# Two overlapped attention branches on one core: fewer filler matmuls, a signal per score matmul, and work of the last stage moved forward

## The chip, the cores and the metric

One core of one Trainium2 chip. The metric is device time of one execution in microseconds. The kernel before takes 1512.03 us (median of 4, 1510.74 to 1512.83).

The engines: PE multiplies matrices, DVE is the vector engine, ACT the scalar engine (exponentials), POOL a third elementwise engine, SP issues DMAs. In this kernel each has a list of instructions of its own, and one waits for another through semaphores.

## The reference, cut

Two branches on separate inputs, both with S = 2048, D = 512, 32 heads of 16.

```python
def _A_ref(x, wqkv, wo):              # ordinary softmax attention
    q, k, v = ...                     # x @ wqkv, split in heads
    scores = jnp.einsum("bhqd,bhkd->bhqk", q, k) * Dh ** -0.5
    p = _softmax(scores, axis=-1)
    o = jnp.einsum("bhqk,bhkd->bhqd", p, v)
    return o.reshape(B, S, D) @ wo

def _B_ref(x, wqkv, w_phi, wo):       # linear attention with learned feature maps
    q, k, v = ...
    pq, pk = q @ w_phi, k @ w_phi     # per head, 16 x 16
    phi_q = concat([softmax(pq), softmax(-pq)]); phi_k = the same of pk
    kv = einsum("bhsf,bhsd->bhfd", phi_k, v);  z = phi_k summed over s
    o = (phi_q @ kv) / (phi_q @ z + 1e-6)
    return o.reshape(B, S, D) @ wo

out = concat([A, B], axis=-1)
```

## The kernel before

**The loop.** Branch A runs in 1024 slots, 32 to a unit (a group of four heads and 512 queries). A slot does two things for different units: the first pass, two score matmuls (L561) and DVE's row-max over 128 x 1024 of them (L573); and, 43 slots later, the second pass, two score matmuls with the maximum folded in (L642), ACT's exponential of each (L654), and every other slot four P·V matmuls (L669). The second pass has three score banks in PSUM.

```python
def emit_m2(B):
    n, bank, dep = ring_next()                     # one of banks 4, 5, 6
    m2_t[B] = P.op("pe", lambda e: e.matmul(PS[:, bank, :], KT[...], QT[...], ...),
        [dep, qe_t[u], kt_ready[(g, kt // 4)]], signal=(B % 2 == 1))
    if B % 2 == 1:
        m2_t[B - 1] = m2_t[B]                      # both exponentials wait for the second
```

PE also runs `emit_fill`: groups of four matmuls of zeros, which compute nothing. Each slot is filled up to `NCOL = 3` columns of work. Once in a unit, `emit_qb` broadcasts the row maxima through PE into one of the three score banks, for two to three slots; the X copy empties the P·V bank; and ACT does two Ln and two Exp of the denominators.

```python
for tau in range(last_slot + 1):
    if tau < total_q1: emit_m1(tau)                # first pass
    ... emit_m2, emit_exp of slot tau - 43 ...     # second pass
    ... P·V, broadcast, hooks of branch B ...
    if tau < total_q1 + LAG and ncol < NCOL:
        emit_fill(NCOL - ncol)
    if tau < total_q1: emit_r1(tau)                # DVE row max
```

**The tail.** In the last 43 slots there is no first pass, so DVE is free. There, hooks (functions tied to a slot) compute branch B's key feature maps, one per 128 rows, three slots apart (`e_k0` to `e_k4`: PE; DVE max, min and two subtractions; ACT exp; DVE sum and reciprocal; POOL product; PE). After the last slot come A's sixteen output projections, a wait on all engines (`endA`), and the final stage: sixteen query feature maps (`q_f0` to `q_f3`, the same arithmetic) in a software pipeline with the query product and B's output projection (`q_s0` to `q_s3`).

```python
for st in range(NKT):
    base = T0 + 3 + 3 * st
    for off, fn in ((0, e_k0), (1, e_k1), (2, e_k2), (3, e_k3), (5, e_k4)):
        tail_hooks.setdefault(base + off, []).append(lambda st=st, fn=fn: fn(st))
...
for st in range(NKT):                              # A's output projection, after attention
    ... 8 matmuls into one bank; copy by ACT or DVE in turn; DMA out ...
endA = [last_tok(k) for k in ("pe", "act", "dve", "pool")]
```

## Time and profile before

| | before |
|---|---|
| loop ends (last row max) | 1282.7 us |
| a unit of 32 slots | 38.01 us |
| tail | 228.4 us |
| of that DVE busy / not busy | 158.7 / 69.6 us |

An engine's reported busy time contains the end of an operation that overlaps the next one's start. Where operations follow one another without a wait, the spacing of their starts is what one costs: a row max is reported at 1.22 us and costs 1.131; a 512-column exponential is reported at 0.60 and costs 0.49. In a timeline line, the first column is the start, the second the stretch covered by the "x" operations named at its end, and the bracket the idle time before them with what ended it. PEclk is the granted PE clock as a share of full.

### The profile page before, as it was taken

To read this page: it belongs to the slowest core of one execution; us is meant where nothing else is said; L and a number is where in the kernel's file an instruction comes from. 1 tells how busy PE (TensorE), PEld (TensorE's weight loads), DVE (VectorE), ACT (ScalarE), POOL (GpSimd) and SP (SyncE) were. 2 spreads that over 40 slices of the span, in tenths; PEclk is the share of its full clock that TensorE was granted. 3 is DMA by queue.
4 is the path that set the end of the run, shared out by engine and by line. 5 is a ranking of instruction groups with operands and counts; after the bars stand their busy time and mean duration, and the time that the engine had idled before them with its cause. 6 is when DMAs were issued, how large, how long until landed. Compare 5 with 4: busy or idle time off the path is not lost.

```text
span 1511.1 us, 40934 instructions
## 1 busy us (share of the span) xinstructions
PE 1404.6 (93%) x18220; PEld 468.5 (31%) x18220; DVE 1353.5 (90%) x1341; ACT 1301.8 (86%) x2466; POOL 157.0 (10%) x257
## 2 busy tenths in 40 slices
PE   3999999999999999999999999999999999897766
PEld 1433333333333333333333333333333333332333
DVE  3399999999999999999999999999999999575598
ACT  2648999999999999999999999999999999883256
POOL 4000000000000000000000000000000000243143
PEclk9999999999999999999999999999999999997879
DMA  5006000000000000000000000000000000000101
GB/s 111 1 1 127 20 5 6 5 6 5 5 5 6 5 5 5 5 5 6 5 5 5 6 6 5 5 6 5 6 5 5 5 5 5 5 2 15 46 18 39
DMA packets 34513, 20.47 MB, mean 14 GB/s; under 512 B 25120, under 2 KB 31776, under 8 KB 34336
## 3 DMA queue, kind: packets, MB, share of 16 engines
q1 hardware_dynamic: 34336, 17.86, 5.4%
q8 instruction: 142, 2.33, 0.6%
q14 instruction: 35, 0.29, 0.1%
HBM read 4.21 MB, written 4.19 MB: 6 GB/s over the span
## 4 chain that ended last, share of the span: by engine, by line
PE 75%; ACT 13%; DVE 9%; SPq 2%; issue 1%; POOL 0%; DMA 0%; DVEq 0%; ACTq 0%; POOLq 0%
PE PS L685 31%; PE PS L561 19%; ACT pT L654 10%; PE PS L669 9%; PE PS L642 5%; PE PS L274 4%; PE PS L804 2%; DVE part L573 2%; SPq L174 1%; DVE VP L421 1%; PE PS L696 1%; ACT ebK L412 1%; ACT X L706 1%; PE PS L256 1%; PE PS L391 1%
## 5 line engine op out<-in xcount | busy, mean ns | idle before, releaser
L573 DVE TENSOR_REDUCE part<-PS 128x2 f32<-128x1024 f32 x1024 | 1181.9, 1219 | 82.5 <-PE PS L561 55.4
L654 ACT ACTIVATE pT<-PS 128x512 bf16<-128x512 f32 x2048 | 1115.7, 600 | 51.9 <-PE PS L642 39.8
L685 PE MATMUL PS<-zmv,ones_t 128*32 128x512 bf16 x9176 | 665.8, 381 | 0.0
L642 PE MATMUL PS<-QT,KT 32*128 32x512 bf16 x2048 | 464.8, 385 | 11.7 <-ACT pT L654 5.7
L561 PE MATMUL PS<-KT,QT 32*128 32x512 bf16 x2048 | 397.4, 385 | 0.1
L685 PEld LDWEIGHTS PS<-zmv,ones_t 128*32 128x32 bf16 x9176 | 205.0, 96 | 199.4 <-issue 101.4
L561 PEld LDWEIGHTS PS<-KT,QT 32*128 32x128 bf16 x2048 | 96.4, 91 | 430.4 <-issue 256.5
L669 PE MATMUL PS<-pT,VP 128*32 128x512 bf16 x2048 | 205.0, 390 | 13.3 <-ACT X L706 13.3
L642 PEld LDWEIGHTS PS<-QT,KT 32*128 32x128 bf16 x2048 | 124.8, 91 | 66.1 <-ACT pT L654 37.5
L730 POOL TENSOR_TENSOR QT<-X,Yd 128x256 bf16<-128x256 f32 x64 | 46.5, 727 | 786.4 <-ACT Yd L728 786.4
L669 PEld LDWEIGHTS PS<-pT,VP 128*32 128x32 bf16 x2048 | 52.6, 92 | 131.7 <-issue 109.4
L274 PE MATMUL PS<-xAT,WKp 128*128 128x512 bf16 x128 | 35.0, 416 | 22.8 <-DVE WKp L197 17.2
L286 ACT ACTIVATE KT<-PS,bias_k 128x512 bf16<-128x512 f32 x32 | 22.0, 687 | 37.4 <-PE PS L274 37.4
L696 PE MATMUL PS<-zmv,ones_t 128*32 128x512 bf16 x692 | 49.7, 381 | 3.2
L594 POOL TENSOR_SCALAR stage<-mrow 128x16 bf16<-128x16 f32 x32 | 9.9, 310 | 407.9 <-DVE mrow L584 407.9
L378 ACT ACTIVATE VP<-PS 128x1024 bf16<-128x1024 bf16 (+2 forms) x33 | 25.9, 789 | 18.8 <-PE PS L899 15.0
L433 POOL TENSOR_TENSOR QT<-KT,VP 128x512 bf16<-128x512 bf16 x32 | 33.1, 1056 | 80.3 <-DVE VP L424 43.4
L391 PE MATMUL PS<-WKp,xAT 128*128 128x512 bf16 x128 | 39.9, 448 | 0.0
L433 POOL TENSOR_TENSOR phikK<-ebK,statK 128x512 bf16<-128x512 bf16 x32 | 33.1, 1056 | 64.3 <-DVE statK L424 51.2
L282 ACT ACTIVATE QT<-PS 128x512 bf16<-128x512 f32 x32 | 19.1, 597 | 20.9 <-PE PS L274 20.9
L421 DVE TENSOR_REDUCE statK<-ebK 128x64 f32<-128x1024 bf16 x16 | 19.5, 1220 | 18.7 <-ACT ebK L412 18.7
L274 PE MATMUL PS<-xAT,WQp 128*128 128x512 bf16 x128 | 34.0, 389 | 0.0
(79 smaller groups left out, 646.4 us busy)
## 6 DMA issues: line engine op xcount, KB each, us to landing
Yd<-X SPq DMA_DIRECT2D x128, 32.0 KB, 2.0
out_dram<-OA SPq DMA_DIRECT2D x16, 128.0 KB, 1.7
out_dram<-pT SPq DMA_DIRECT2D x16, 128.0 KB, 1.7
wA<-in_A_wqkv_dram SPq DMA_DIRECT2D x3, 512.0 KB, 4.4
wA<-in_B_wqkv_dram SPq DMA_DIRECT2D x1, 1536.0 KB, 8.6
WOp<-in_A_wo_dram SPq DMA_DIRECT2D x4, 128.0 KB, 6.4
BD<-in_B_w_phi_dram SPq DMA_DIRECT2D x32, 0.5 KB, 1.5
woB<-in_B_wo_dram SPq DMA_DIRECT2D x1, 512.0 KB, 4.6
```

Source lines behind the costliest of these rows:

```text
L274: tok = P.op("pe", lambda e, ct=ct: e.matmul(PS[:, b, :], wpad[:, ct, g, :], xAT[:, ct, c * 512:(c + 1) * 512], start=(ct == 0), stop=(ct ...
L391: tok = bank_task(bank, 4, lambda e, b, ct: e.matmul(PS[:, b, :], xBT[:, ct, st * 128:(st + 1) * 128], Wf[:, x, ct, :], start=(ct == 0), s ...
L421: t6 = P.op("dve", lambda e: e.tensor_reduce(ss, ebuf[:, ie, :].rearrange("p (g f) -> p g f", f=16), AX.X, ALU.add), [ctx["exp"]] + users. ...
L433: t8 = P.op("pool", lambda e, a=a: e.tensor_tensor(dv[:, a], ev4[:, a], rs3[:, a].unsqueeze(2).broadcast_to([128, 32, 16]), ALU.mult), [ct ...
L561: tok = P.op("pe", lambda e, r=r: e.matmul(PS[:, r, :], QT[32 * r:32 * r + 32, g, q0:q0 + 128], KT[32 * r:32 * r + 32, g, kc * 512:(kc + 1 ...
L573: r1[q1] = P.op("dve", lambda e: e.tensor_reduce(part[:, u % 2, qt, 2 * half:2 * half + 2, kc], PS[:, 2 * half:2 * half + 2, :], AX.X, ALU ...
L642: m2_t[B] = P.op("pe", lambda e: e.matmul(PS[:, bank, :], KT[32 * r:32 * r + 32, g, kt * 128:(kt + 1) * 128], QT[32 * r:32 * r + 32, g, c ...
L654: exp_t[B] = P.op("act", lambda e: e.activation(pT[:, slot, :], PS[:, bank, :], ACT.Exp, scale=0.25), [m2_t[B], slot_reader.get(slot)])
L669: tok = P.op("pe", lambda e, B=B, r=r: e.matmul(PVB[32 * r:32 * r + 32, :], VP[:, kt, 4 * g + r, :], pT[:, B % RING, :], start=(kt == 0), ...
L685: P.op("pe", lambda e, cq=cq: e.matmul(PVB[32 * cq:32 * cq + 32, :], ones_t[:, 0:32], zmv[:, :], start=False, stop=False, tile_position=(0 ...
L696: P.op("pe", lambda e, cq=cq: e.matmul(PS[32 * cq:32 * cq + 32, bank, :], ones_t[:, 0:32], zmv[:, :], start=True, stop=True, tile_position ...
L730: t = P.op("pool", lambda e: e.tensor_tensor(QT[:, g, lo:lo + 256], X[:, ub, sl], Yd[:, ub, sl], ALU.mult), [ex, xev_t[u], last_m2[u]])
```

## The change

Two small edits in the loop and several in the tail. The intent, in its own words, is to overlap early query feature maps of branch B and A's output projection with attention.

```diff
-    NCOL = 3
+    NCOL = 2
...
-                wB[:], B_wqkv.rearrange(...)), done)                    # B's weights: only the value third
+                wB[:, :, 1024:1536], B_wqkv.rearrange(...)[:, :, 1024:1536]), done)
...
-            ctx["v"] = P.op("act", lambda e: e.activation(               # value copy of a key map
+            ctx["v"] = P.op("dve", lambda e: e.tensor_copy(
...
+        NEQ = 12                      # e_q0..e_q3: twelve query maps, in the key maps' buffers
+        ...                           # their results wait in parts of wB, WQp, phikK, vBK
+        def e_oproj(st): ...          # one output projection; the copy always on DVE
...
-            for off, fn in ((0, e_k0), (1, e_k1), (2, e_k2), (3, e_k3), (5, e_k4)):
+            for off, fn in ((0, e_k0), (1, e_k1), (4, e_k2), (5, e_k3), (7, e_k4)):
+        for j in range(NEQ):
+            base = T0 + 3 + 3 * NKT + 3 * j
+            ...
+        for st in range(12):
+            tail_hooks.setdefault(T0 + 5 + 3 * st, []).append(lambda st=st: e_oproj(st))
+        for st in range(12, 16):
+            tail_hooks.setdefault(32 * (NU - 1) + 90 + 2 * (st - 12), [])...
...
-                [dep, qe_t[u], kt_ready[(g, kt // 4)]], signal=(B % 2 == 1))
+                [dep, qe_t[u], kt_ready[(g, kt // 4)]])                  # every score matmul signals
-                m2_t[B - 1] = m2_t[B]
...
-                ncol += 2                                                # the broadcast's columns
+                ncol += 3
...
-            if tau < total_q1 + LAG and ncol < NCOL:
+            if tau < total_q1 and ncol < NCOL:                           # no fills in the tail
...
-        for st in range(NKT): ...     # the sixteen projections after attention: gone from here
...                                    # q_f0..q_f3 skip st < NEQ and take the early result
```

More of the change, by code (lines that the diff above doesn't have):

```diff
@@ L344, in b_loads @@
             BL["wb"] = P.dma("sp", d_wb, lambda e: e.dma_start(
-                wB[:], B_wqkv.rearrange("(ct p) n -> p ct n", p=128)), done)
+                wB[:, :, 1024:1536], B_wqkv.rearrange("(ct p) n -> p ct n", p=128)[:, :, 1024:1536]), done)
             for x in range(2):
@@ L387, in e_fold, with fm0 @@
             return 1
-        def fm0(st, x, tbuf, sbuf, ctx, bank):
+        def fm0(st, x, tbuf, sbuf, ctx, bank, rk="E"):
             i = ctx["i"]
@@ L396, in fm0 @@
             mn = sbuf[:, i, 32:64]
-            prev = users.get(("mxmn", x, i), []) + users.get(("tb", x, i), [])
+            ctx["rk"] = rk
+            prev = users.get(("mxmn", rk, i), []) + users.get(("tb", rk, i), [])
             t1 = P.op("dve", lambda e: e.tensor_reduce(mx, pv, AX.X, ALU.max), [tok] + prev)
@@ L405, in fm0 @@
             bank_reader[bank] = t4
-            users[("mxmn", x, i)] = [t3, t4]
+            users[("mxmn", rk, i)] = [t3, t4]
             ctx["sub"] = [t3, t4]
@@ L412, in fm1 @@
             ctx["exp"] = P.op("act", lambda e: e.activation(ebuf[:, ie, :], tbuf[:, i, :], ACT.Exp),
-                              ctx["sub"] + users.get(("eb", x, ie), []))
-            users[("tb", x, i)] = [ctx["exp"]]
+                              ctx["sub"] + users.get(("eb", ctx["rk"], ie), []))
+            users[("tb", ctx["rk"], i)] = [ctx["exp"]]
         def fm2(x, ebuf, sbuf, ctx):
@@ L422, in fm2 @@
                 ss, ebuf[:, ie, :].rearrange("p (g f) -> p g f", f=16), AX.X, ALU.add),
-                [ctx["exp"]] + users.get(("ssrs", x, i), []))
+                [ctx["exp"]] + users.get(("ssrs", ctx["rk"], i), []))
             ctx["rs"] = P.op("dve", lambda e: e.reciprocal(rs, ss), [t6])
@@ L435, in fm3 @@
                     [ctx["rs"]] + after)
-            users[("ssrs", x, i)] = [t8]
-            users[("eb", x, ctx["ie"])] = [t8]
+            users[("ssrs", ctx["rk"], i)] = [t8]
+            users[("eb", ctx["rk"], ctx["ie"])] = [t8]
             ctx["phi"] = t8
@@ L447, in e_k0 @@
             vv = vBK[:, st % 4, :].rearrange("p (h j) -> p h j", j=17)
-            ctx["v"] = P.op("act", lambda e: e.activation(
-                vv[:, :, 0:16], PS[:, b, :].rearrange("p (h d) -> p h d", d=16), ACT.Copy),
+            ctx["v"] = P.op("dve", lambda e: e.tensor_copy(
+                vv[:, :, 0:16], PS[:, b, :].rearrange("p (h d) -> p h d", d=16)),
                 [tok, t_vb1] + users.get(("v", st % 4), []))
@@ L481, in e_k4, with e_q0, e_q1, e_q2 @@
             return 1
+        NEQ = 12
+        wTf = WQp[:].rearrange("p a b c -> p (a b c)")
+        vBf = vBK[:].rearrange("p a n -> p (a n)")
+        phiq_slot = {}
+        for j in range(4):
+            phiq_slot[j] = wB[:, j, 0:1024]
+            phiq_slot[4 + j] = wTf[:, 1024 * j:1024 * (j + 1)]
+        phiq_slot[8] = phikK[:, 0, :]
+        phiq_slot[9] = phikK[:, 1, :]
+        phiq_slot[10] = vBf[:, 0:1024]
+        phiq_slot[11] = vBf[:, 1024:2048]
+        qst = {}
+        def e_q0(j):
+            f = NKT + j
+            ctx = qst.setdefault(j, {"i": f % 2, "ie": f % 3})
+            fm0(j, 0, tbK, statK, ctx, early_bank())
+            return 1
+        def e_q1(j):
+            fm1(0, tbK, ebK, qst[j])
+            return 0
+        def e_q2(j):
+            fm2(0, ebK, statK, qst[j])
+            return 0
+        def e_q3(j):
+            after = []
+            if j >= 4:
+                after = list(wf_tok.values())
+            if j >= 8:
+                after = [kst[NKT - 1]["kv"]]
+            fm3(0, ebK, statK, qst[j], phiq_slot[j], after)
+            return 0
+        OA = sb("OA", [128, 2, 512], BF)
+        d_oa = [dsem("oa0"), dsem("oa1")]
+        oa_t = {}
+        def e_oproj(st):
+            c = st // 4
+            b = early_bank()
+            deps = [mul_t[u] for u in range(NU) if units[u][1] == c] + [t_wo, bank_reader.get(b)]
+            tok = None
+            for g in range(NG):
+                tok = P.op("pe", lambda e, g=g: e.matmul(
+                    PS[:, b, :], QT[:, g, st * 128:(st + 1) * 128], WOp[:, g, :],
+                    start=(g == 0), stop=(g == NG - 1)), deps if g == 0 else [], signal=(g == NG - 1))
+            t = P.op("dve", lambda e: e.tensor_copy(OA[:, st % 2, :], PS[:, b, :]), [tok, oa_t.get(st - 2)])
+            bank_reader[b] = t
+            oa_t[st] = P.dma("sp", d_oa[st % 2], lambda e: e.dma_start(
+                out[0][st * 128:(st + 1) * 128, 0:512], OA[:, st % 2, :]), [t])
+            return 2
         tail_hooks = {}
@@ L491, in bass_concat_heads__softmax_full_mha__linear_kernel_hedgehog__prompt_kernel @@
             base = T0 + 3 + 3 * st
-            for off, fn in ((0, e_k0), (1, e_k1), (2, e_k2), (3, e_k3), (5, e_k4)):
+            for off, fn in ((0, e_k0), (1, e_k1), (4, e_k2), (5, e_k3), (7, e_k4)):
                 tail_hooks.setdefault(base + off, []).append(lambda st=st, fn=fn: fn(st))
+        for j in range(NEQ):
+            base = T0 + 3 + 3 * NKT + 3 * j
+            for off, fn in ((0, e_q0), (1, e_q1), (4, e_q2), (5, e_q3)):
+                tail_hooks.setdefault(base + off, []).append(lambda j=j, fn=fn: fn(j))
+        for st in range(12):
+            tail_hooks.setdefault(T0 + 5 + 3 * st, []).append(lambda st=st: e_oproj(st))
+        for st in range(12, 16):
+            tail_hooks.setdefault(32 * (NU - 1) + 90 + 2 * (st - 12), []).append(lambda st=st: e_oproj(st))
         part = sb("part", [128, 2, 4, 4, NKC], F32)
@@ L793, in bass_concat_heads__softmax_full_mha__linear_kernel_hedgehog__prompt_kernel @@
                 fn()
-        OA = sb("OA", [128, 2, 512], BF)
-        d_oa = [dsem("oa0"), dsem("oa1")]
-        oa_t = {}
-        for st in range(NKT):
-            c = st // 4
-            b = ser_bank()
-            deps = [mul_t[u] for u in range(NU) if units[u][1] == c] + [t_wo, bank_reader.get(b)]
-            tok = None
-            for g in range(NG):
-                tok = P.op("pe", lambda e, g=g, b=b, st=st: e.matmul(
-                    PS[:, b, :], QT[:, g, st * 128:(st + 1) * 128], WOp[:, g, :],
-                    start=(g == 0), stop=(g == NG - 1)), deps if g == 0 else [], signal=(g == NG - 1))
-            t = evac(OA[:, st % 2, :], PS[:, b, :], [tok, oa_t.get(st - 2)])
-            bank_reader[b] = t
-            oa_t[st] = P.dma("sp", d_oa[st % 2], lambda e, st=st: e.dma_start(
-                out[0][st * 128:(st + 1) * 128, 0:512], OA[:, st % 2, :]), [t])
         endA = [last_tok(k) for k in ("pe", "act", "dve", "pool")]
@@ L839, in q_f0 @@
         def q_f0(st, ctx):
+            if st < NEQ:
+                return
             ctx["i"] = st % 2
             ctx["ie"] = st % 3
-            users[("tb", 0, ctx["i"])] = users.get(("tb", 0, ctx["i"]), []) + (endA if st < 2 else [])
-            fm0(st, 0, tbQ, statQ, ctx, ser_bank())
+            users[("tb", "L", ctx["i"])] = users.get(("tb", "L", ctx["i"]), []) + endA
+            fm0(st, 0, tbQ, statQ, ctx, ser_bank(), "L")
         def q_f1(st, ctx):
-            users[("eb", 0, ctx["ie"])] = users.get(("eb", 0, ctx["ie"]), []) + (endA if st < 3 else [])
+            if st < NEQ:
+                return
+            users[("eb", "L", ctx["ie"])] = users.get(("eb", "L", ctx["ie"]), []) + endA
             fm1(0, tbQ, ebQ, ctx)
         def q_f2(st, ctx):
+            if st < NEQ:
+                return
             fm2(0, ebQ, statQ, ctx)
         def q_f3(st, ctx):
-            fm3(0, ebQ, statQ, ctx, phiq[:, st % NR, :], users.get(("phiq", st % NR), []) + endA)
+            if st < NEQ:
+                ctx["phi"] = qst[st]["phi"]
+                return
+            phiq_slot[st] = phiq[:, st % NR, :]
+            fm3(0, ebQ, statQ, ctx, phiq_slot[st], endA)
         def q_s0(st, ctx):
@@ L858, in q_s0 @@
             tok = bank_task(b, 8, lambda e, b, t: e.transpose(
-                PS[:, b, :].bitcast(BF)[:, t * 128:(t + 1) * 128], phiq[:, i, t * 128:(t + 1) * 128], ident[:, :]),
-                [ctx["phi"], t_ident])
-            users[("phiq", i)] = [tok]
+                PS[:, b, :].bitcast(BF)[:, t * 128:(t + 1) * 128], phiq_slot[st][:, t * 128:(t + 1) * 128],
+                ident[:, :]), [ctx["phi"], t_ident])
             ctx["pt"] = aevac(phiqT[:, i].rearrange("p t s -> p (t s)"), PS[:, b, :].bitcast(BF),
```

## The prediction

> **What bounds the kernel now.** I read the page first, busy shares and slices.
>
> ```profile
> PE 1404.6 (93%) x18220; PEld 468.5 (31%) x18220; DVE 1353.5 (90%) x1341; ACT 1301.8 (86%) x2466; POOL 157.0 (10%) x257
> ...
> PE   3999999999999999999999999999999999897766
> ...
> DVE  3399999999999999999999999999999999575598
> ...
> PEclk9999999999999999999999999999999999997879
> ...
> L573 DVE TENSOR_REDUCE part<-PS 128x2 f32<-128x1024 f32 x1024 | 1181.9, 1219 | 82.5 <-PE PS L561 55.4
> ```
>
> Three engines look full, so shares do not choose. There are two stages: a loop of 1024 slots (one row-max reduction on DVE, two exponentials on ACT, two score pairs and "fill" matmuls on PE per slot) up to about 1283 us, and a tail of 228 us where the slices thin out. So I asked for DVE's timeline over one unit of 32 slots.
>
> ```profile
> 600.68 0.21 DVE L584 TENSOR_REDUCE mrow<-part 128x16 f32<-128x64 f32 x1
> 600.81 8.00 DVE L573 TENSOR_REDUCE part<-PS 128x2 f32<-128x1024 f32 x7
> 609.11 1.23 DVE L573 TENSOR_REDUCE part<-PS 128x2 f32<-128x1024 f32 x1 [0.30 <-PE PS L561]
> 610.67 6.89 DVE L573 TENSOR_REDUCE part<-PS 128x2 f32<-128x1024 f32 x6 [0.33 <-PE PS L642]
> 617.94 20.84 DVE L573 TENSOR_REDUCE part<-PS 128x2 f32<-128x1024 f32 x18 [0.38 <-PE PS L642]
> 638.69 0.21 DVE L584 TENSOR_REDUCE mrow<-part 128x16 f32<-128x64 f32 x1
> ```
>
> Seven reductions take 8.00 us, each reported 1.22: starts lie (8.00-1.22)/6 = 1.13 us apart. A unit lasts 638.69-600.68 = 38.01 us, against 32 x 1.131 = 36.19. The missing 1.82 us, by start spacing: 0.39 and 0.43 before 609.11 and 610.67 (the row-max broadcast, L604/L611, holds one of three score banks), 0.48 before 617.94 (P·V waits for X to leave its bank), 0.39 in the run of 18 (17 spacings take 19.62, not 19.23; the Ln/Exp pairs of the normalisation), 0.13 for the mrow reduction. So DVE is the floor, and 1.69 us a unit is PE arriving late. ACT's own cost shows in the same unit:
>
> ```profile
> 606.46 1.08 ACT L654 ACTIVATE pT<-PS 128x512 bf16<-128x512 f32 x2 [0.47 <-PE PS L642]
> 607.43 0.39 ACT L622 ACTIVATE QT<-PS 128x256 bf16<-128x256 f32 x1
> 608.02 1.08 ACT L654 ACTIVATE pT<-PS 128x512 bf16<-128x512 f32 x2 [0.20 <-PE PS L642]
> ```
>
> Two exponentials in 1.08 at about 0.595 each: 0.49 apart, 0.97 a slot. ACT has slack; its 86% counts overlap. PE has almost none: an undisturbed slot is four row-tiled matmuls, 0.31 us to the first fill, three fills 0.22 apart, 0.32 to the next score: 1.09 of 1.13 us.
>
> [...] matmuls of 512 columns start 0.22 us apart where the granted clock is 1.00 and 0.43 apart at 0.50, and the granted clock of the tail changes as below. [...]
>
> ```profile
> 1282.05:1288.88 6.83, 5.24 (x68) 2.54 (x64) 0.91 (x2) 6.83 (x14) 0.85 (x3) 1.00 0.00 0
> 1288.88:1295.71 6.83, 6.46 (x31) 2.00 (x32) 0.97 (x2) 3.85 (x8) 0.00 (x0) 0.50 0.01 2
> 1295.71:1312.77 17.06, 15.42 (x191) 5.50 (x190) 12.12 (x18) 14.72 (x27) 4.49 (x5) 1.00 0.01 1
> ```
>
> **The change, part by part.**
>
> *Fills 3 to 2.* One fill group is 0.216 us, so PE's slot falls to 1.09-0.22 = 0.87 us. PE then waits for DVE: a score pair starts as soon as its bank is free, about 1.0 us before its reduction, and needs 0.43 to deliver. PE can run some 0.57 us late before DVE starves, where it has 0 to 0.3 now.
>
> *Each P·V score matmul (L642) signals.* Today the first exponential of a pair waits for the second matmul. While the broadcast holds a bank, the second starts 0.22 us later (the 0.47 idle above), then 0.47 later. I walked the broadcast slots by hand with these durations: with both edits the score issue falls behind by 0.17, 0.18 and 0.33 us, under 0.57: no starvation. With two fills but paired signals it would be about 0.45 us short by the third slot, so the signal matters. For X: P·V is held 0.60, the next scores come 0.33 late: absorbed. For Ln/Exp: four slots add 0.31 us of ACT each to 0.97, a backlog of 0.6, minus 0.06 of bank slack and 0.26 of PE slack: absorbed. Left is 0.13 a unit. Bound on the gain: from slot 43 on, the spacing beyond 1.131 sums to 54.6 us; less 31 x 0.126 = 3.9 leaves 50.7. I take 45, some residue staying. The first 40 slots carry projections, not fills, and stay.
>
> *Tail.* Before, from the end of the last reduction (1282.7): 12.0 us to the first key feature map on DVE, 16 of those about 5.7 us apart, 30 us of A's output projection with DVE nearly idle, then 92 us of query features, bound by DVE:
>
> ```profile
> 1387.74 29.53 PE L804 MATMUL PS<-WOp,QT 128*128 128x512 bf16 x128
> ...
> 1417.31 0.69 DVE L226 CAST OA<-PS 128x512 bf16<-128x512 f32 x1 [2.76 <-PE PS L804]
> ...
> 1441.39 0.68 DVE L398 TENSOR_REDUCE VP<-PS 128x32 f32<-128x512 f32 x1
> ...
> 1446.78 0.68 DVE L398 TENSOR_REDUCE VP<-PS 128x32 f32<-128x512 f32 x1
> ```
>
> The last two are a step of 5.39: four 512-column operations of 0.60, a sum of 1.24, a reciprocal of 0.47, together 4.11, and 1.28 after the query product. Moving a query map does not remove its 4.11 us; only DVE's idle time can be won. After:
> - Start to first key map: 11 us (folds the same, fills gone).
> - Key maps 0-12 beside attention and 12 projections. DVE: 2.4+1.7 + value copy 0.6 (moved from ACT) + projection copy 0.6 = 5.3. PE: three score pairs 1.0, P·V 0.5, key and value matmuls 1.8, key-value product 0.4, projection 1.8 = 5.5. I take 5.8: 13 x 5.8 = 75.
> - Key maps 13-15, attention over, DVE alone: 3 x 4.75 = 14.
> - Early query maps: the attention slots end at 1066 and their first hook is 1077, so in spite of the title they run after attention: 12 x 4.11 + 4 x 0.6 = 52, plus 2.5 for the last Pool product before the barrier.
> - Final stage: set-up 1.3; 8 steps without features at ACT's 1.95 (copies 0.9+0.5+0.5) less their ramp, 14; [...] steps 12-17 by DVE (3.7+3.7+5.4+5.4+3.0+3.0) 24; drain and store 8. About 50.
>
> Sum 11+75+14+54.5+50 = 205 against 228: 23 won, I take 22.
>
> Total: 1512 - 45 - 22 = **1445 us**.
>
> **Rivals.** (a) [...] Streaming time in a slot becomes about 0.28 + 2 x 0.216 = 0.71 of 1.13 us, 63%. By my count of starts the tail has windows of 63 to 66% that stay at full clock; those followed by a drop had under half. So I expect full clock. If it fell, PE's slot would be 1.5 us or more; [...] the loop gains nothing, about 1490. (b) *ACT becomes the bound*: its pair is 0.97; I see no place for it beyond single slots, but if backlogs meet, half the 50.7 stays: about 1467. (c) *The tail gives nothing*: projection and value copies lengthen the key maps to 7 us each, PE blocked by in-order waits; then 13 x 1.2 = 16 us of the 22 go: about 1461. (d) *The smaller weight load* (a third of the columns) is hidden under the loop: nothing. (e) Only the moves matter and the loop stays: 1490; against it speak the 1.69 us a unit of PE lateness.
>
> **Range and chances.** The loop gives 25 to 51, the tail 8 to 34; both low ends together are unlikely. 8 in 10: 1428 to 1470. Two per cent is 1482; missing it needs (a), or (b) with (c). Faster 0.94, same 0.05, slower 0.01.
>
> **What would show it.** Right: reductions 1.13 us apart with only the 0.13 per unit left, a unit of about 36.4 us, last reduction ending near 1238; PEclk at 9 through the loop; projection lines between key maps, no 30 us block; twelve query maps about 4.1 us apart after attention; a final stage near 50 us. Wrong: PEclk under 9 in the loop; reductions still waiting on L642; key maps over 6.5 us apart with PE waiting for Pool or ACT.

## The result, and the profile after

The changed kernel takes 1442.36 us (median of 8, 1440.18 to 1442.81) against 1511.44 for the kernel before (13 runs). The ratio is 0.9538 (0.9528 to 0.9547): 4.6% faster. Ratios here are the mean time of one kernel's runs over that of the other's runs of the same rounds, so not quite the ratio of the medians quoted.

The page of the changed kernel: busy shares, then the slices, then the row-max group.

```profile
PE 1254.6 (87%) x14028; PEld 373.1 (26%) x14028; DVE 1349.5 (94%) x1365; ACT 1256.1 (87%) x2442; POOL 156.8 (11%) x257
...
DVE  3299999999999999999999999999999999599988
...
PEclk9999999999999999999999999999999999898759
...
L637 DVE TENSOR_REDUCE part<-PS 128x2 f32<-128x1024 f32 x1024 | 1164.6, 1211 | 48.9 <-PE PS L625 46.5
```

PE has 4192 matmuls less and its share fell from 93 to 87%, while PEclk stayed at 1.00 in the loop (from 33 to 1234 us). DVE does the same work in a shorter span. The waits before the row max fell from 82.5 to 48.9 us. Summed from the trace's records, all of that remainder lies before the first 43 row maxima, while the kernel starts up. Later there is none, as in DVE's timeline over a little more than one unit:

```profile
599.83 17.05 DVE L637 TENSOR_REDUCE part<-PS 128x2 f32<-128x1024 f32 x15
616.80 0.21 DVE L648 TENSOR_REDUCE mrow<-part 128x16 f32<-128x64 f32 x1
616.93 23.84 DVE L637 TENSOR_REDUCE part<-PS 128x2 f32<-128x1024 f32 x21
```

Before, a unit broke into four runs of row maxima, three of them after a wait named in brackets (the lines are in the prediction). Now there is no bracket at all: (17.05 - 1.22)/14 and (23.84 - 1.22)/20 are both 1.131 us. Only the 0.13 us of the mrow reduction, which joins the partial maxima of a unit, is left, and the unit is 36.33 us. The last row max ends at 1232.15 instead of 1282.74: **50.6 us** come from the loop.

The tail went from 228.4 to 208.5 us: **19.8 us**. Busy time by stretch, in the columns length, PE, PEld, DVE, ACT, POOL (each with its count of instructions), PEclk, DMA share, GB/s. First the kernel before: start of the tail, key maps, projections, final stage.

```profile
1282.74:1294.74 12.00, 10.03 (x91) 3.89 (x81) 0.22 (x2) 9.99 (x20) 0.85 (x3) 0.76 0.00 1
1294.74:1384.60 89.86, 75.43 (x1002) 27.10 (x1000) 67.03 (x95) 67.52 (x118) 32.43 (x32) 0.94 0.02 5
1384.60:1419.08 34.48, 31.67 (x170) 14.17 (x171) 6.76 (x12) 5.06 (x9) 3.43 (x4) 0.90 0.18 60
1419.08:1511.10 92.02, 55.47 (x440) 32.10 (x438) 84.74 (x177) 50.30 (x64) 33.12 (x32) 0.81 0.07 24
```

Then the changed kernel: start, key maps 0 to 12, key maps 13 to 15, early query maps up to POOL's last product, final stage.

```profile
1232.15:1242.88 10.73, 9.12 (x58) 4.10 (x58) 0.23 (x2) 9.13 (x19) 0.84 (x3) 0.61 0.01 2
1242.88:1318.31 75.43, 74.28 (x730) 28.39 (x728) 66.83 (x101) 53.93 (x94) 24.18 (x24) 0.99 0.08 24
1318.31:1332.24 13.93, 10.07 (x116) 3.41 (x116) 13.82 (x22) 4.27 (x6) 6.21 (x6) 0.56 0.05 11
1332.24:1391.03 58.79, 27.39 (x156) 9.79 (x156) 52.65 (x79) 13.29 (x14) 30.27 (x30) 0.65 0.03 9
1391.03:1440.69 49.66, 37.43 (x384) 24.83 (x384) 38.29 (x105) 36.96 (x53) 8.28 (x8) 0.89 0.13 43
```

The DVE column tells the tail: 158.7 us of work in 228.4 before, 171.8 in 208.5 after. DVE got 13.1 us more to do (the value copies and more of the projection copies) and lost 32.9 us of time in which it was not busy. The stretch of 34.5 us in which DVE worked 6.8 is gone.

### The profile page after: what moved, and what is told of

It reads as the page before. It is cut to its first block, busy times and chain, and to the rows that moved or that the text cites.

```text
span 1440.7 us, 32535 instructions
## 1 busy us (share of the span) xinstructions
PE 1254.6 (87%) x14028; PEld 373.1 (26%) x14028; DVE 1349.5 (94%) x1365; ACT 1256.1 (87%) x2442; POOL 156.8 (11%) x257
## 4 chain that ended last, share of the span: by engine, by line
DVE 83%; PE 13%; SPq 2%; ACT 1%; issue 1%; POOL 1%; DMA 0%; DVEq 0%; ACTq 0%; POOLq 0%
DVE part L637 77%; PE PS L274 4%; PE PS L530 2%; SPq L174 1%; PE PS L706 1%; DVE statK L422 1%; PE PS L391 1%; PE PS L256 1%; PE PS L625 1%; PE PS L445 1%; DVE tbK L404 1%; DVE statK L400 1%; DVE statK L399 1%; PE PS L966 1%; DVE statK L425 0%
## 5 line engine op out<-in xcount | busy, mean ns | idle before, releaser
L637 DVE TENSOR_REDUCE part<-PS 128x2 f32<-128x1024 f32 x1024 | 1164.6, 1211 | 48.9 <-PE PS L625 46.5
L717 ACT ACTIVATE pT<-PS 128x512 bf16<-128x512 f32 x2048 | 1088.3, 604 | 49.9 <-PE PS L706 26.9
L706 PE MATMUL PS<-QT,KT 32*128 32x512 bf16 x2048 | 504.0, 385 | 7.7 <-ACT pT L717 0.8
L748 PE MATMUL PS<-zmv,ones_t 128*32 128x512 bf16 x5260 | 442.1, 383 | 0.0
L706 PEld LDWEIGHTS PS<-QT,KT 32*128 32x128 bf16 x2048 | 139.4, 91 | 84.1 <-ACT pT L717 60.0
L748 PEld LDWEIGHTS PS<-zmv,ones_t 128*32 128x32 bf16 x5260 | 100.2, 95 | 97.0 <-issue 97.0
L413 ACT ACTIVATE ebK<-tbK 128x1024 bf16<-128x1024 f32 x28 | 29.6, 1057 | 54.0 <-DVE tbK L404 54.0
L434 POOL TENSOR_TENSOR phikK<-ebK,statK 128x512 bf16<-128x512 bf16 x36 | 37.2, 1056 | 71.6 <-DVE statK L425 57.1
L759 PE MATMUL PS<-zmv,ones_t 128*32 128x512 bf16 x416 | 34.4, 383 | 2.5
L399 DVE TENSOR_REDUCE statK<-PS 128x32 f32<-128x512 f32 x28 | 18.6, 666 | 16.8 <-PE PS L391 16.8
L422 DVE TENSOR_REDUCE statK<-ebK 128x64 f32<-128x1024 bf16 x28 | 33.9, 1209 | 0.0
```

The source lines that it names most:

```text
L422: t6 = P.op("dve", lambda e: e.tensor_reduce(ss, ebuf[:, ie, :].rearrange("p (g f) -> p g f", f=16), AX.X, ALU.add), [ctx["exp"]] + users. ...
L434: t8 = P.op("pool", lambda e, a=a: e.tensor_tensor(dv[:, a], ev4[:, a], rs3[:, a].unsqueeze(2).broadcast_to([128, 32, 16]), ALU.mult), [ct ...
L637: r1[q1] = P.op("dve", lambda e: e.tensor_reduce(part[:, u % 2, qt, 2 * half:2 * half + 2, kc], PS[:, 2 * half:2 * half + 2, :], AX.X, ALU ...
L706: m2_t[B] = P.op("pe", lambda e: e.matmul(PS[:, bank, :], KT[32 * r:32 * r + 32, g, kt * 128:(kt + 1) * 128], QT[32 * r:32 * r + 32, g, c ...
L717: exp_t[B] = P.op("act", lambda e: e.activation(pT[:, slot, :], PS[:, bank, :], ACT.Exp, scale=0.25), [m2_t[B], slot_reader.get(slot)])
L748: P.op("pe", lambda e, cq=cq: e.matmul(PVB[32 * cq:32 * cq + 32, :], ones_t[:, 0:32], zmv[:, :], start=False, stop=False, tile_position=(0 ...
```

## The experiments

Twelve kernels, all correct. The loop's end and the tail are from each kernel's profiled run (the last row max's end; the span from there). "Ratio" is against the kernel before in the same rounds.

| run | median us | ratio (95%) | loop ends | tail |
|---|---|---|---|---|
| before | 1511.4 | | 1282.7 | 228.4 |
| the change | 1442.4 | 0.9538 (0.9528-0.9547) | 1232.2 | 208.5 |
| loop_fills | 1493.7 | 0.9882 (0.9866-0.9899) | 1257.8 | 232.2 |
| loop_signal | 1496.8 | 0.9895 (0.9880-0.9910) | 1266.8 | 228.4 |
| loop_both | 1466.2 | 0.9697 (0.9683-0.9712) | 1232.9 | 232.0 |
| tail_only | 1493.7 | 0.9876 (0.9861-0.9890) | 1282.1 | 208.4 |
| early0 | 1442.0 | 0.9538 (0.9523-0.9552) | 1231.2 | 208.8 |
| early8 | 1439.3 | 0.9516 (0.9502-0.9531) | 1231.9 | 206.0 |
| fill1 | 1503.2 | 0.9941 (0.9921-0.9962) | 1298.5 | 209.2 |
| fill0 | 1558.0 | 1.0300 (1.0283-1.0317) | 1347.4 | 209.1 |
| oproj_end | 1475.8 | 0.9756 (0.9741-0.9770) | 1232.9 | 239.2 |
| joined6 | 1430.2 | 0.9456 (0.9440-0.9472) | 1232.1 | 196.9 |
| joined4 | 1430.9 | 0.9460 (0.9446-0.9474) | 1232.2 | 197.1 |
| joined6v | 1430.0 | 0.9455 (0.9440-0.9469) | 1232.1 | 196.9 |

### The two loop edits, apart and together

**loop_fills**: the kernel before with the fills alone.

```diff
-    NCOL = 3
+    NCOL = 2
-                ncol += 2        # broadcast
+                ncol += 3
```

> The kernel before with two fill groups instead of three (and the broadcast counted as three), signals and tail as before. My theory: both loop edits are needed. PE gains 0.22 us a slot, so the stalls at X (0.48 us a unit) and at Ln/Exp (0.38) go; at the row-max broadcast the exponential still waits for the second matmul of its pair and about 0.45 of the 0.82 us stays. Unit 36.3 + 0.5 = 36.8 us, total 1511 - 30 x 1.2 = about 1475 us. Rival: PE room alone was missing, the signal is ornament: unit 36.3, total 1461 us.

The second line changes nothing here: with `NCOL = 2`, a slot with a broadcast gets no fill whether the broadcast counts as two columns or three.

**loop_signal**: the kernel before with the signal alone.

```diff
-                ..., signal=(B % 2 == 1))
+                ...)
-                m2_t[B - 1] = m2_t[B]
```

> The kernel before with a signal on every second-pass score matmul, three fills and the tail as before. My theory: in the broadcast slots the exponentials start 0.22 us earlier, which by hand turns 0.39 + 0.43 lost into about 0.17 + 0.18; X and Ln/Exp stay, as PE still needs 1.09 of 1.13 us. Gain 0.5 us a unit, total about 1495 us. Rival 'signal does nothing without room': 1511 us. Rival 'the signal is the whole loop gain': 1461 us.

**loop_both**: both edits, old tail.

> The kernel before with both loop edits and its old tail. My theory: the loop's 50.6 us seen between the two traces come from these edits alone: 1461 us, unit 36.33 us, PEclk full. Rival 'moving work out of the tail also helps the loop': slower than 1470 us.

DVE's timeline in loop_signal, over the broadcast, the X copy and the Ln/Exp pairs of one unit:

```profile
599.34 11.73 DVE L573 TENSOR_REDUCE part<-PS 128x2 f32<-128x1024 f32 x10
611.43 20.80 DVE L573 TENSOR_REDUCE part<-PS 128x2 f32<-128x1024 f32 x18 [0.36 <-PE PS L642]
```

The same in loop_fills:

```profile
600.27 6.88 DVE L573 TENSOR_REDUCE part<-PS 128x2 f32<-128x1024 f32 x6 [0.34 <-PE PS L561]
607.38 20.48 DVE L573 TENSOR_REDUCE part<-PS 128x2 f32<-128x1024 f32 x18 [0.22 <-PE PS L642]
```

With the signal alone, the wait at X stays (0.36 idle before 611.43) and so does the loss in the run of 18, where the Ln/Exp pairs lie: (20.80 - 1.22)/17 is 1.152. The broadcast now hides in the run of ten: (11.73 - 1.22)/9 is 1.168. With the fills alone it is the other way round: the run of 18 is nearly clean, 1.133 apart, but the broadcast still costs 0.34 and X 0.22 of idle time. Summed over the starts of all row maxima, in us beyond 1.131 per unit (mean of 28 units):

| | broadcast | X | Ln/Exp | mrow |
|---|---|---|---|---|
| before | 0.83 | 0.48 | 0.38 | 0.13 |
| loop_signal | 0.33 | 0.46 | 0.35 | 0.13 |
| loop_fills | 0.53 | 0.32 | 0.02 | 0.13 |
| loop_both, and the change | 0 | 0 | 0 | 0.13 |

So the edits address different waits, and together they give more than their sum: the loop ends 16.0 us earlier with the signal, 24.9 with the fills, 49.9 with both. The rival "one of them is the whole gain" is refuted from both sides. loop_signal is close to my hand count (0.33 against 0.35 at the broadcast, 1496.8 against 1495). **loop_fills missed**: I expected 1475 us, as I took the X wait for gone with the fills alone. It kept 0.32 of 0.48, some 10 us over the loop; the tail, 3.8 us longer, and 0.08 us a unit more at the broadcast make up most of the rest. My count had used the exponentials' starts of the kernel with both edits. The X copy stands behind them in ACT's order, and the traces show that paired signals delay it too: counted from the start of the row max three places before the one that waits, it starts at 2.06 us in loop_fills, 1.99 in loop_signal, 2.02 before, and 1.57 with both edits (means of 28 units, which differ by 0.01 at most).

loop_fills and loop_both also have a tail 3.6 to 3.8 us longer than before. That turned out to belong to the clock (a mean PEclk of 0.89 over loop_both's key maps against 1.00 before), below.

### The tail edits alone

**tail_only**: the changed kernel with three fills and paired signals put back.

> The changed kernel with three fill groups and paired signals put back: the tail edits alone. My theory: the two parts add up, so 1511 - 20 = 1491 us, loop units of 38.0 us. Rival 'the tail edits only pay together with the faster loop': 1505 us or more. Rival 'the tail is the larger half': 1470 us.

Loop as before (1282.1), tail as after (208.4 us). The tail edits are worth 20 us whether the loop is fast or slow. In the other direction they do interact a little: with two fills the old tail takes 232.0, so added to loop_both they are worth 23.5.

### How many fills PE needs

**fill1** and **fill0**: the changed kernel with `NCOL = 1` and `NCOL = 0`.

> The changed kernel with one fill group instead of two. By my count of starts PE streams 0.28 + 0.22 of 1.13 us, 44%[...]. My theory: the clock falls and recovers in turns in the loop, PEclk 0.6 to 0.9 there, and some of the slack is spent: 1445 to 1475 us. Rival 'fills are only load, fewer is better': 1442 us or less and the clock stays.

> The changed kernel without fills. 25% busy at full clock, about 50% at half clock: my theory: PE stays at half clock through the loop. Plain slots still fit 1.13 us, but matmuls take 0.22 us longer to deliver, and the broadcast and X stalls come back at 1 to 2 us a unit: 1475 to 1510 us. Rival 'DVE bounds even at half clock': 1442 us.

The slices of fill1's page:

```profile
PEclk9999557777985555557778955555577779798759
```

Of fill0's page:

```profile
PEclk9995555555555555555555555555555555599759
```

And two stretches of fill1's loop (columns as above):

```profile
400.00:430.00 30.00, 23.23 (x232) 7.06 (x229) 30.00 (x28) 29.36 (x59) 2.24 (x5) 1.00 0.03 6
450.00:520.00 70.00, 69.25 (x477) 17.10 (x476) 65.61 (x57) 63.15 (x125) 3.74 (x7) 0.50 0.02 5
```

With one group of matmuls of zeros less the kernel loses 61 us, with two less 116. The number of fills is the only edit, so it is the fills that hold the clock up: PEclk is 1.00 in the loop of the change, 0.5 in 14 of the 34 slices of fill1's loop, and from the fourth slice to the end of the loop in fill0's. The reported busy share does not show it: in the first stretch PE is reported busy 77% at full clock, in the second 99% at half clock, and it stays there for 70 us. DVE, fully busy in the first stretch, waits in the second.

The starts of the matmuls say more. I count 512 columns as 0.216 us at full clock, the spacing of fills in a row, and as twice that at half clock (0.427 apart between 1288.88 and 1295.70 us before the change, where PEclk is 0.50). I count in intervals of 3.41 us: the traces before and after have the clock at 1.00 or 0.50, in stretches such as 3.41, 6.83, 10.24 and 75.09 us, and 3.41 is the shortest that the program's end does not cut off. The change then streams for 60 to 77% of each interval around 600 to 640 us (50 to 82% over the loop from 150 us on), at PEclk 1.00. fill1 streams for 37 to 40% of the intervals after 117 us, at full clock for some 30 us, and then loses it. In its second stretch above it streams for 72 to 85% of each interval, at half clock, and the clock stays down. From this no share can be given that keeps the clock: in the tails before and after the change, single intervals of 38 to 41% were at full clock and so was the next (0.38 from 1469.8 us before; 0.41 from 1354.0 and 0.40 from 1415.5 us after). fill1 also scatters more than any other run (1492.5 to 1513.5 over 15). Both were slower than I expected (1503 against 1445 to 1475, 1558 against 1475 to 1510): that a fall of the clock in the loop would be short was my estimate, which no run had shown. In fill1 it often is not: from 222.9 to 298.0 us it has the full clock for 17 us and half of it for 20.5 by turns, and from 536.9 us it has half of it for 150 us.

So the rival "a fill is only load" is refuted, and the prediction's rival (a), the clock falling, is real one step further on. Two groups are the best of the four values tried, three being loop_signal's loop.

### The early query maps

**early0** and **early8**: none or eight early maps instead of twelve. (Late maps get places of their own in QT, as there are more than four.)

```diff
-        NEQ = 12
+        NEQ = 0          # or 8
-            phiq_slot[st] = phiq[:, st % NR, :]
+            phiq_slot[st] = qtf[:, 1024 * st:1024 * (st + 1)]
```

> The changed kernel with no early query map (12 set to 0; late maps get own places in QT): the twelve maps go back to the final stage. My theory: they ran after attention in any case, on the engine that bounds, so DVE's work is the same and only its idle stretches move: the end of the last key map at 1336, a wait for the last projections of about 10 us, then the old final stage of 92: about 1437 us, within 1430 to 1446. Rival, the change's own intent: the early maps save what the final stage lost from 92 to 53 us, so undoing them costs some 35 us: about 1475 us.

> The changed kernel with eight early query maps instead of twelve. My theory: flat, 1440 us within 5, since a map costs DVE the same 4.1 us early or late. Rival 'each early map saves 3 us': 1454 us.

1442.0 us without any, 1439.3 with eight, 1442.4 with twelve. **The part of the change that its description names first is worth nothing**, and twelve are some 3 us slower than eight (all eight runs of the change are slower than all four of early8, but they come from different rounds, and the intervals of the two ratios just touch). The early maps' hooks lie behind the last attention slot, so they run after attention, on DVE, which bounds there anyway. What moved is where DVE stands idle. In early0 it is here, in the order of time on DVE, at the projections that still come after attention:

```profile
1332.03 0.55 DVE L425 RECIPROCAL statK<-statK 128x64 f32<-128x64 f32 x1
1340.14 0.69 DVE L533 CAST OA<-PS 128x512 bf16<-128x512 f32 x1 [7.56 <-PE PS L530]
```

In the changed kernel it is at the wait for all engines (ACT's copy, which ends the 2.94 us below, had itself waited for POOL's last product) and in the steps of the final stage without maps:

```profile
1387.97 0.55 DVE L425 RECIPROCAL statK<-statK 128x64 f32<-128x64 f32 x1
1391.46 0.73 DVE L878 TENSOR_TENSOR VP<-VP,qmask 128x544 bf16<-128x544 f32 x1 [2.94 <-ACT VP L378]
1392.84 0.40 DVE L939 TENSOR_SCALAR VP<-PS 128x16 f32<-128x16 f32 x2 [0.66 <-PE PS L927]
```

Over the whole tail DVE is not busy for 38.1 us of 208.8 in early0 and 36.7 of 208.5 in the change.

### A's output projection beside attention

**oproj_end**: early0 with all sixteen projections behind attention.

```diff
-        for st in range(12):
-            tail_hooks.setdefault(T0 + 5 + 3 * st, [])...
-        for st in range(12, 16):
-            tail_hooks.setdefault(32 * (NU - 1) + 90 + 2 * (st - 12), [])...
+        for st in range(16):
+            tail_hooks.setdefault(32 * (NU - 1) + 90 + 2 * st, [])...
```

> The changed kernel with no early query maps and all sixteen output projections after attention again, so that of the tail edits only the later reductions, the value copy on DVE and the missing tail fills stay. Against the run without early maps (1442.0 us). My theory: the projections beside attention cost the key maps PE time and DVE 0.6 us each, so without them the key maps come some 4.8 us apart instead of 5.77 (about 13 us won over fifteen), while twelve more projections stand alone, some 20 us lost: about 1449 us. Rival 'overlapping the projection is the whole 24 us between this tail and the old one': about 1466 us.

1475.8 us, 34 more than early0, where I expected 7. **My theory was wrong here.** I expected the key maps to come faster with less work beside them. They came slower: the first to the last start 96.7 us apart instead of 84.2, and the projections behind attention cost another 19. The key-map stage of oproj_end:

```profile
1242.00:1326.00 84.00, 68.01 (x574) 22.64 (x584) 56.40 (x84) 50.43 (x92) 24.21 (x24) 0.73 0.01 3
```

The same stretch of early0:

```profile
1242.00:1326.00 84.00, 76.28 (x795) 30.40 (x807) 75.82 (x115) 56.52 (x97) 28.30 (x28) 0.99 0.08 23
```

The mean clock is 0.73 instead of 0.99, and DVE is busy 56 us instead of 76. The tail has no fills any more; the projections took their place. They are useful work and also keep PE's clock up: 0.99 with them, 0.73 without. The old tail shows the same, weaker, with two fills (loop_both) against three (before):

```profile
1243.00:1324.00 81.00, 66.75 (x751) 23.17 (x762) 55.31 (x79) 59.80 (x108) 26.91 (x27) 0.89 0.01 3
1295.00:1370.00 75.00, 66.94 (x890) 24.08 (x888) 55.60 (x80) 61.45 (x108) 26.71 (x27) 1.00 0.02 3
```

loop_both's tail is 3.6 us longer. The single steps from one key map to the next tie the loss to the clock. In loop_fills and loop_both, the 7 of 24 steps with full clock throughout took 5.5 to 6.0 us (mean 5.8), the other 17 took 5.7 to 7.2 (mean 6.4). In oproj_end the one step with full clock took 5.99 us, not the 4.8 I had expected, and the other eleven 6.2 to 7.6 (mean 7.0). With three fills, as before the change and also without projections beside attention, the clock stays at 1.00 and the twelve steps take 5.77 us on average.

### A version that uses this

What is left to win is DVE's idle time. **joined6** has six early maps to bridge the end of attention; spreads the last four projections between them, three slots apart, with their copies on ACT; gives the late maps the early maps' buffers and places in KT; and replaces the wait for all engines by waits for the last readers of what is overwritten.

```diff
-        NEQ = 12
+        NEQ = 6
-            tail_hooks.setdefault(32 * (NU - 1) + 90 + 2 * (st - 12), [])...
+            tail_hooks.setdefault(32 * (NU - 1) + 92 + 3 * (st - 12), [])...
+            # in e_oproj, st >= 12: the copy by ACT
-        endA = [last_tok(k) for k in ("pe", "act", "dve", "pool")]
+        endA = [pv_t[(NU - 1, NKT - 1)], last_m2[NU - 1], qe_t[NU - 1], xev_t[NU - 1], r1[total_q1 - 1]]
-            fm0(st, 0, tbQ, statQ, ctx, ser_bank(), "L")
+            fm0(st, 0, tbK, statK, ctx, ser_bank())        # and so q_f1, q_f2, q_f3
```

> A version of mine: six early query maps; the last four projections spread between them three slots apart with their copies on ACT; the late maps use the early maps' buffers and places in KT, and the final stage waits only for the last readers of what it overwrites, not for all four engines. My theory: what is left to win in the tail is DVE's idle time: 3 us at the projections after attention, about 4.5 us at the barrier, 9 us in the steps without maps, 2.4 us of copies. Expected 1427 us, 1422 to 1433. Rival 'DVE's order does not matter, drains and PE's clock eat it': 1438 us or more.

**joined4** has four early maps. **joined6v** is joined6 with the value copy of the key maps back on ACT.

> The same with four early maps. My theory: within 3 us of six early maps (about 1428 us), as only DVE's idle time counts; a little slower if PE's last two projections stand before the first late map. Rival 'each early map saves 3 us': 6 us slower.

> Six early maps joined as above, and the value copy back on ACT, as it was before the change. My theory: beside attention the key maps are paced by PE in order (5.77 us), so DVE's 0.6 us there is free, and only the three maps after attention gain: 2 us faster than joined6. Rival 'DVE bounds all sixteen': 9 us faster. Rival 'ACT blocks on the value matmuls': slower.

joined6 takes 1430.2 us, ratio 0.9456 against the change's 0.9538, intervals apart: it beats both kernels, by 5.4 and 0.9%. Its DVE is not busy for 28.0 us of a tail of 196.9. Its four edits were not run one by one, so what each is worth is not shown. At the place where the change waited 2.94 us, DVE's timeline of joined6 now has this:

```profile
1358.42 0.55 DVE L425 RECIPROCAL statK<-statK 128x64 f32<-128x64 f32 x1
1358.89 1.14 DVE L881 TENSOR_TENSOR VP<-VP,qmask 128x544 bf16<-128x544 f32 x1
1360.60 0.40 DVE L940 TENSOR_SCALAR VP<-PS 128x16 f32<-128x16 f32 x2 [0.57 <-PE PS L928]
```

I expected 1427; the result is inside the range of 1422 to 1433 that I gave. joined4 is level with it (1430.9), as expected: the number of early maps does not matter in itself. joined6v is level too (1430.0), where I expected 2 us less. Its maps after attention are faster (4.05 to 4.12 us apart instead of 4.64 to 4.71), and those beside attention slower (5.88 instead of 5.78), which about cancels. Why they are slower beside attention was not tested.

## Why the prediction was right, point by point

The time was predicted as 1445 us and measured as 1442.4, well inside 1428 to 1470. That it came so close is in part luck: the loop gave 5.6 us more than the 45 taken, the tail 2.2 us less than the 22, and the two errors partly cancel. The steps:

1. **DVE's row max is the floor of the loop and PE's lateness the loss.** Right. The spacing 1.131 us did not move, and all 1.69 us a unit of PE's lateness went.
2. **The loop's gain.** I bounded it at 50.7 us and took 45, "some residue staying". There was no residue: 50.6. The walk by hand (0.33 us late at most, 0.57 allowed) was good enough to be trusted; the discount was not.
3. **The signal matters.** Right: with two fills and paired signals, 0.53 us a unit stays at the broadcast (0.45 by hand). The 1024 signals added show no cost: the row maxima stay 1.131 us apart. That X and Ln/Exp would be absorbed is right for both edits together; applied to the fills alone in an expectation, it was wrong for X.
4. **The clock stays full at about 63% streaming.** Right: PEclk is 1.00 over the loop, and a count of starts gives 67% on average. The evidence I gave, that the intervals of 3.41 us before a drop had under half (0 to 38% in the tail before), does not say which share is enough: others of 38 to 41% were followed by no drop. With one group fewer, in fill1, the clock did not stay full (0.50 from 450 to 520 us). My estimate that a fall would be short was wrong: fill1 stays at half clock for 70 us and more.
5. **The tail by stretches**, predicted and measured: start 11 and 10.7; key maps 0 to 12, 75 and 75.4; key maps 13 to 15, 14 and 13.9; early query maps 54.5 and 58.8; final stage 50 and 49.7. The mis-sized term is the early maps. The thirteenth projection waits on PE for attention's last product and stands ahead of a query map, so DVE waits 2.27 and 0.51 us around 1343, with PE at half clock up to there (PEclk 0.50 from 1319.9 to 1343.8; and 0.41 at 1336.8); and the sum and reciprocal of the last key map, 1.7 us, fall into this stretch, as its hooks now come one map later.
6. **"Moving a query map does not remove its 4.11 us."** Right, and stronger than I used it: early0 shows that the whole part is worth nothing.
7. **What made the tail shorter.** I credited it to DVE's idle time beside the projections, which is right in sum (32.9 us less idle, 13.1 us more work). I did not see that the projections also replace the fills that the change takes out of the tail. Without both, the tail is 239 us, longer than the old one.

The rivals: (a) did not happen with two fills, and happens with one; (b), ACT as the bound, is excluded by the loop's lack of any wait; (c), key maps 7 us apart, was not seen (5.78, after a first step of 7.2, whose first 1.9 us were at half clock); (d), the smaller load, is hidden: loop_both loads all of the weights and has the same 36.33 us unit as the change; (e) is refuted by loop_both and tail_only.

Open: what the granted clock follows, as neither the busy share nor the share of a single interval tells it here; and what an early query map truly beside attention would give, as DVE has only some 8.6 us to spare in that stage (66.8 busy of 75.4) and no run tried it.

## What to carry to other kernels

When an engine is the floor of a loop, look at the starts of its operations, not its busy share: the sum of the spacings beyond the floor is an exact bound on what the other engines can still cost, and a wait of a few tenths can need two edits before it goes. Filler matmuls were here both load and clock (PEclk 1.00 in the loop with two groups, 0.50 for 70 us and more with one): try how many keep the clock, keep that many, and when real work can take the fillers' place, as the projections did here, it pays twice. Moving the query maps earlier gained nothing, as the engine that does them was not idle there; check in which slot the moved hooks in fact run.
